# Where the weights begin: a three-pass fp32r loop with its weight tiles moved to multiples of 128 bytes

## The chip, the cores and the metric

One core of one Trainium2 chip runs one program: an attention over 12,480 rows with 32 inducing points, and two multi-layer perceptrons behind it. The metric is the time of one execution on the device, in microseconds (us). The kernel before took 996.77 us as the median of 3 runs (994.26 to 998.2).

An address in this document is the byte at which a tile begins within a partition of SBUF, the on-chip memory. "32 past" means that this address leaves 32 when it is divided by 128.

## The reference, cut to what matters

```python
def _attn_ref(x, inducing):              # x: 1 x 12480 x 128, inducing: 32 x 128
    def mab(q, kv):
        s = scale * (q @ kv.transpose(0, 2, 1))
        a = np.exp(s - s.max(-1, keepdims=True))
        a /= a.sum(-1, keepdims=True) + 1e-09
        return a @ kv
    h = mab(I, x)                        # 32 x 128
    return mab(x, h)                     # 12480 x 128
def _moe_ref(x, w_in, w_out, alpha):     # w_in: 128 x 2048, w_out: 2048 x 128
    h = x @ w_in
    g = np.maximum(h, 0.0) + alpha * np.minimum(h, 0.0)
    return g @ w_out
def _moe2_ref(x, w_in, w_out):
    h = np.maximum(x @ w_in, 0.0)
    return h * h @ w_out
# out = _moe2_ref(_moe_ref(_attn_ref(x, inducing)))
```

## The kernel before, in words

The rows are cut into 30 tiles of 416. A first part (about the first 60 us) loads x, transposes it into `xT`, computes the first attention over all rows and prepares the weights. Then comes the main loop, one step for each pair of a tile of rows and one of the 16 chunks of 128 hidden units, 480 steps, with three layers of it at work on different tiles at the same time.

In each step TensorE runs ten matmuls on 416 moving columns:

- `l1_a` (L570), one matmul: weights `w1s`, moving `a_s`. Its result goes through a Relu on ScalarE (L574) and a split into a high and a low part, `g1h` and `g1l` (L576, VectorE).
- `l1_b` (L580 to L582 in `three`), three matmuls: `wo_hi` with `g1h`, `wo_lo` with `g1h`, `wo_hi` with `g1l`.
- `l2_a` (the same three lines), weights `w2i_hi` and `w2i_lo`, moving `y1h` and `y1l`.
- `l2_b` (the same three lines), weights `w2o_hi` and `w2o_lo`, moving `g2h` and `g2l` (L620 on ScalarE, L622 on GpSimd).

Once for each tile of rows one more matmul follows (L597, weights `v_s`), and once for every four tiles the second attention puts in its scores (L432). All matmuls of the main loop are in fp32r, a form of fp32 that needs one pass; in the first part fp32 is used, in which each matmul that isn't a transpose stands twice in the trace. Each matmul has its own weight load (PEld in the profile): 128 columns of 4 bytes, thus 512 bytes of each partition, and 416 x 4 = 1,664 bytes of each partition move past it. The order on every engine is that in which the code is written (`manual_schedule`); no planner changes it.

Where the tiles lie follows from the order in which the pool `keep` hands them out. `xT` begins 32 past and has 49,920 bytes, which is 390 x 128. So `w1s` behind it begins 32 past, and as each weight tile has 8,192 bytes (64 x 128), `wo_hi`, `wo_lo`, `w2i_hi`, `w2i_lo`, `w2o_hi` and `w2o_lo` all do; a chunk of 128 columns has 512 bytes, so that each single weight load begins 32 past too. In the first part the last four of these places hold `w_in_sb`, `w_out_sb`, `wiT` and `aw`. `v_s` and `hT` behind them are 32 past as well. The moving tiles (`a_s`, `g1h`, `g1l`, `y1h`, `y1l`, `g2h`, `g2l`) have 1,664 bytes each, 13 x 128, and all begin 64 past, as `ident` does.

The names that the prediction speaks of: `keep_tile` (L63), the place of `xT` and `w1s` (L95 to L102), `make_identity` and `same` on GpSimd (L77 to L86), `three` (L579 to L582).

Of the kernel before, what the change touches and what calls it, by code (L numbers as in the profile page):

```python
# [9 lines left out]
F32 = mybir.dt.float32  # L10
# [15 lines left out]
def attention_then_two_mlps(ctx: ExitStack, tc, x, inducing, w_in, w_out, alpha, w2_in, w2_out, out):  # L26
# [3 lines left out]
    nc = tc.nc  # L30
# [3 lines left out]
    P = 128  # L34
# [6 lines left out]
    keep = ctx.enter_context(tc.tile_pool(name="keep", bufs=1))  # L41
# [21 lines left out]
    def keep_tile(name, shape, dt=F32):  # L63
        return keep.tile(shape, dt, name=name, tag=name)

    f32 = lambda ap: ap.bitcast(F32)


    stage1 = ExitStack()
# [27 lines left out]
    def xt_cols(t):  # L97
        return xT[:, t * T : (t + 1) * T]

    w1s = keep_tile("w1s", [P, DFF], F32R)  # L100
    wo_hi = keep_tile("wo_hi", [P, NCH, P], F32R)
    wo_lo = keep_tile("wo_lo", [P, NCH, P], F32R)  # L102
# [2 lines left out]
    w_out_sb = keep.tile([P, NCH, P], F32, name="w_out_sb", tag="w2i_lo")  # L105
    wiT = keep.tile([P, DFF], F32, name="wiT", tag="w2o_hi")
    aw = keep.tile([P, NCH, P], F32, name="aw", tag="w2o_lo")
    al = keep_tile("al", [P, NCH])
    al1 = keep_tile("al1", [P, NCH])
    v_s = keep_tile("v_s", [P, P], F32R)  # L110
# [144 lines left out]
    nm, e, f, s_g, eT, hb = {}, {}, {}, {}, {}, {}  # L255
# [507 lines left out]
```

## Time and profile before

| | |
|---|---|
| median of 3 runs | 996.77 us (994.26 to 998.2) |
| the profiled execution, its own time | 999.72 us |
| its span, first to last instruction | 996.8 us |
| TensorE matmul, busy | 973.7 us (98%) |
| TensorE weight load, busy | 939.9 us (94%) |
| VectorE / ScalarE / GpSimd, busy | 684.8 / 770.4 / 555.3 us |

The span is 2.9 us shorter than the execution's own time, which has a start and an end around it. Busy TensorE doesn't mean that it works at its peak: the record of one matmul lasts some 350 ns while the next begins after some 187 ns, so matmuls overlap in the trace, and how fast TensorE goes is read from the distance between starts.

### The profile page before, as it was taken

Reading aid. Unit: us, or ns where it says so; the run is one execution under the profiler, and the core shown is the slowest. Engines: PE = TensorE matmul, PEld = TensorE weight load, DVE = VectorE, ACT = ScalarE, POOL = GpSimd, SP = SyncE. Lnnn points to the kernel's source line nnn. Section 1 sums busy time; section 2 is a strip of 40 time slices with the busy share of each in tenths; the row PEclk is TensorE's granted clock in tenths of the full one; section 3 lists DMA queues with packets and bytes.
Section 4 is the critical chain, followed back from the end, with each engine's and each line's share of the span. In section 5 each row is a group of like instructions: output and inputs, shape, how many; then the busy total and the mean of one; then the engine's idle time right before and its main releaser. Section 6 shows DMA issues by size and latency. Waiting matters only on the chain.

```text
span 996.8 us, 16261 instructions
## 1 busy us (share of the span) xinstructions
PE 973.7 (98%) x5423; PEld 939.9 (94%) x5423; DVE 684.8 (69%) x1210; ACT 770.4 (77%) x1607; POOL 555.3 (56%) x518
## 2 busy tenths in 40 slices
PE   7879999999999999999999999999999999999998
PEld 5558999999999999999999999999999999999997
DVE  4688776666766667666776667766677666776667
ACT  4569877777887778877787778877787777787776
POOL 1256966555665556655565555655556555565530
PEclk9889999999999999999999999999999999999999
DMA  8715002000020000100001000010000100010001
GB/s 220 200 56 149 1 9 44 10 7 4 10 44 10 10 1 10 44 10 10 3 10 42 10 9 10 10 35 10 9 9 18 27 10 9 10 27 1 10 9 18
DMA packets 66289, 28.42 MB, mean 29 GB/s; under 512 B 54205, under 2 KB 62061, under 8 KB 66205
## 3 DMA queue, kind: packets, MB, share of 16 engines
q1 hardware_dynamic: 66205, 27.39, 12.1%
q8 instruction: 42, 0.69, 0.3%
q14 instruction: 42, 0.34, 0.1%
HBM read 14.80 MB, written 6.39 MB: 21 GB/s over the span
## 4 chain that ended last, share of the span: by engine, by line
PE 91%; DMA 3%; DVE 2%; ACT 2%; issue 1%; POOL 0%; SPq 0%; ACTq 0%; POOLq 0%; DVEq 0%
PE y L582 18%; PE y L581 18%; PE y L580 17%; PE h L582 9%; PE h L581 9%; PE h L580 9%; PE h L570 9%; DMA xg<-in_x_dram 3%; PE ms L432 1%; PE y L597 1%; PE h L236 0%; DMA raw<-in_moe_w_out_dram 0%; ACT g1h L574 0%; DVE mag L175 0%; DVE g1l L576 0%
## 5 line engine op out<-in xcount | busy, mean ns | idle before, releaser
L622 POOL TENSOR_TENSOR g2l<-sq,g2h 128x416 fp32r<-128x416 f32 x456 | 496.2, 1089 | 343.9 <-ACT g2h L620 206.5
L576 DVE SCALAR_TENSOR_TENSOR g1l<-h,g1h 128x416 fp32r<-128x416 f32 x480 | 282.6, 589 | 221.7 <-ACT g1h L574 217.2
L574 ACT ACTIVATE g1h<-h 128x416 fp32r<-128x416 f32 x480 | 248.3, 518 | 132.9 <-PE h L570 129.9
L614 DVE TENSOR_TENSOR sq<-h,r 128x416 f32<-128x416 f32 x480 | 283.6, 591 | 52.2 <-ACT r L612 3.8
L612 ACT ACTIVATE r<-h 128x416 f32<-128x416 f32 x480 | 249.5, 520 | 53.6 <-PE h L582 7.7
L620 ACT CAST g2h<-sq 128x416 fp32r<-128x416 f32 x480 | 255.6, 532 | 2.3 <-DVE sq L614 2.1
L570 PE MATMUL h<-a_s,w1s 128*128 128x416 f32 (+1 forms) x480 | 170.4, 356 | 4.2 <-DVE g1l L576 2.9
L582 PE MATMUL y<-g2l,w2o_hi 128*128 128x416 f32 x480 | 168.7, 351 | 0.3 <-POOL g2l L622 0.3
L582 PE MATMUL y<-g1l,wo_hi 128*128 128x416 f32 x480 | 168.3, 351 | 0.0
L580 PE MATMUL h<-y1h,w2i_hi 128*128 128x416 f32 x480 | 168.1, 350 | 0.2
L582 PE MATMUL h<-y1l,w2i_hi 128*128 128x416 f32 x480 | 167.9, 350 | 0.2 <-DVE y1l L601 0.2
L581 PE MATMUL y<-g1h,wo_lo 128*128 128x416 f32 x480 | 168.0, 350 | 0.0
L581 PE MATMUL h<-y1h,w2i_lo 128*128 128x416 f32 x480 | 168.0, 350 | 0.0
L581 PE MATMUL y<-g2h,w2o_lo 128*128 128x416 f32 x480 | 168.0, 350 | 0.0
L580 PE MATMUL y<-g1h,wo_hi 128*128 128x416 f32 x480 | 167.7, 349 | 0.0
L580 PE MATMUL y<-g2h,w2o_hi 128*128 128x416 f32 x480 | 167.5, 349 | 0.0
L570 PEld LDWEIGHTS h<-a_s,w1s 128*128 128x128 f32 (+1 forms) x480 | 90.5, 189 | 12.0 <-DVE g1l L576 5.7
L580 PEld LDWEIGHTS h<-y1h,w2i_hi 128*128 128x128 f32 x480 | 90.0, 188 | 2.8 <-DVE sq L614 1.4
L580 PEld LDWEIGHTS y<-g1h,wo_hi 128*128 128x128 f32 x480 | 90.3, 188 | 1.0 <-issue 0.5
L582 PEld LDWEIGHTS y<-g2l,w2o_hi 128*128 128x128 f32 x480 | 90.1, 188 | 1.2 <-POOL g2l L622 0.7
L581 PEld LDWEIGHTS y<-g2h,w2o_lo 128*128 128x128 f32 x480 | 90.1, 188 | 0.9 <-POOL w2o_lo L181 0.3
L581 PEld LDWEIGHTS y<-g1h,wo_lo 128*128 128x128 f32 x480 | 90.3, 188 | 0.5
(127 smaller groups left out, 761.4 us busy)
## 6 DMA issues: line engine op xcount, KB each, us to landing
out_dram<-o SPq DMA_DIRECT2D x120, 52.0 KB
xg<-in_x_dram SPq DMA_DIRECT2D x13, 416.0 KB
raw<-in_moe_w_in_dram SPq DMA_DIRECT2D x8, 512.0 KB
raw<-in_moe_w_out_dram SPq DMA_DIRECT2D x8, 512.0 KB
a_s<-a_hi SPq DMA_DIRECT2D x58, 52.0 KB
a_s<-a_lo SPq DMA_DIRECT2D x58, 52.0 KB
xg<-in_x_dram SPq DMA_DIRECT2D x4, 208.0 KB
ind<-in_inducing_dram SPq DMA_DIRECT2D x1, 16.0 KB
```

Of the source, the lines that this page charges most:

```text
L432: nc.tensor.matmul(b[i * M : (i + 1) * M, :w], hT[:, :M], rhs, start=True, stop=True, tile_position=(0, i * M),)
L570: nc.tensor.matmul(b[:, :T], w1s[: a.shape[0], c * P : (c + 1) * P], a, start=True, stop=True)
L574: nc.scalar.activation(hi, b[:, :T], AF.Relu)
L576: nc.vector.scalar_tensor_tensor(lo, b[:, :T], 0.0, f32(hi), op0=ALU.max, op1=ALU.subtract)
L580: nc.tensor.matmul(b, w_hi, hi, start=start, stop=False)
L581: nc.tensor.matmul(b, w_lo, hi, start=False, stop=False)
L582: nc.tensor.matmul(b, w_hi, lo, start=False, stop=stop)
L597: nc.tensor.matmul(b, v_s[: a.shape[0]], a, start=False, stop=True)
L612: nc.scalar.activation(r, b, AF.Relu)
L614: nc.vector.tensor_tensor(sq, b, r, op=ALU.mult)
L620: nc.scalar.copy(hi, sq)
L622: (nc.vector if i >= total - LAG2 else nc.gpsimd).tensor_tensor(lo, sq, f32(hi), op=ALU.subtract)
```

## The change

Two tiles that nothing reads are put into the pool `keep`: one of 96 bytes in each partition between `xT` and `w1s`, and one of 32 bytes behind the last weight tile. The first moves all weight tiles up from 32 past to a multiple of 128. Both together make 128 bytes, so that everything behind them (`al`, `v_s`, `hT`, and all tiles of the other pools, the moving ones among them) is moved by 128 and stays where it was within its 128 bytes: `v_s` and `hT` 32 past, the moving tiles 64 past. Each of the two tiles is cleared once by GpSimd.

```diff
     f32 = lambda ap: ap.bitcast(F32)
+    pads = []
+
+    def pad(n, pool=None):
+
+        name = f"pad{len(pads)}"
+        pads.append((pool or keep).tile([P, n // 4], F32, name=name, tag=name))
+        nc.gpsimd.memset(pads[-1], 0.0)
...
+    pad(96)
     w1s = keep_tile("w1s", [P, DFF], F32R)
     wo_hi = keep_tile("wo_hi", [P, NCH, P], F32R)
     wo_lo = keep_tile("wo_lo", [P, NCH, P], F32R)
...
     aw = keep.tile([P, NCH, P], F32, name="aw", tag="w2o_lo")
+    pad(32)
     al = keep_tile("al", [P, NCH])
```

The order on TensorE, VectorE, ScalarE and SyncE is that of before; nine lines are added ahead of the main loop, so that what stood at L570 stands at L579. On GpSimd two instructions are new. This is GpSimd's queue at the start of the program before (`ident` and `same` are masks for the first part, `w_in_sb` is the first weight that is put together):

```order
6 masks.py:197 MEMSET ident 128x128
7 masks.py:199 ISA
8 masks.py:199 AFFINE_SELECT ident<-ident 128x128
9 L81 MEMSET same 128x128
10 L83 AFFINE_SELECT same<-same 128x128 x7
11 L176 TENSOR_TENSOR w_in_sb<-mag,raw 128x512 x4
```

And this is the same place with the change:

```order
6 masks.py:197 MEMSET ident 128x128
7 masks.py:199 ISA
8 masks.py:199 AFFINE_SELECT ident<-ident 128x128
9 L88 MEMSET same 128x128
10 L90 AFFINE_SELECT same<-same 128x128 x7
11 L73 MEMSET pad_109 128x24
12 L73 MEMSET pad_118 128x8
13 L185 TENSOR_TENSOR w_in_sb<-mag,raw 128x512 x4
```

The two clearings stand behind `same` and ahead of the first weight; nothing else has moved.

## Rows read from the trace of the kernel before

**Rows 1.** The page: busy time of TensorE, its granted clock, the chain that ended last.
```profile
PE 973.7 (98%) x5423; PEld 939.9 (94%) x5423; DVE 684.8 (69%) x1210; ACT 770.4 (77%) x1607; POOL 555.3 (56%) x518
...
PEclk9889999999999999999999999999999999999999
...
PE 91%; DMA 3%; DVE 2%; ACT 2%; issue 1%; POOL 0%; SPq 0%; ACTq 0%; POOLq 0%; DVEq 0%
```

**Rows 2.** Busy time in stretches: us, each engine with its instructions (x), clock, DMA.
```profile
0.00:100.00 100.00, 82.01 (x667) 60.53 (x668) 66.48 (x146) 67.10 (x154) 38.30 (x43) 0.93 0.57 156
...
400.00:500.00 100.00, 100.00 (x537) 98.65 (x536) 67.76 (x116) 78.38 (x162) 57.72 (x54) 1.00 0.09 18
500.00:600.00 100.00, 100.00 (x537) 98.66 (x536) 66.73 (x115) 78.14 (x162) 58.86 (x55) 1.00 0.08 16
```

**Rows 3.** Groups of equal shape: weight loads; busy us, mean ns, idle before.
```profile
L580 PEld LDWEIGHTS y<-g1h,wo_hi 128*128 128x128 f32 x480 | 90.3, 188 | 1.0 <-issue 0.5
L570 PEld LDWEIGHTS h<-a_s,w1s 128*128 128x128 f32 x464 | 87.1, 188 | 5.5 <-DVE sq L614 4.1 <-DVE g1l L576 1.1
L597 PEld LDWEIGHTS y<-a_s,v_s 128*128 128x128 f32 x29 | 5.4, 187 | 0.0
```

**Rows 4.** Timeline of TensorE in the loop: start, length (us), what.
```profile
500.11 0.35 PE L570 MATMUL h<-a_s,w1s 128*128 128x416 f32 x1
500.11 0.19 PEld L580 LDWEIGHTS h<-y1h,w2i_hi 128*128 128x128 f32 x1
500.30 0.35 PE L580 MATMUL h<-y1h,w2i_hi 128*128 128x416 f32 x1
500.30 0.19 PEld L581 LDWEIGHTS h<-y1h,w2i_lo 128*128 128x128 f32 x1
500.48 0.35 PE L581 MATMUL h<-y1h,w2i_lo 128*128 128x416 f32 x1
...
500.50 0.52 ACT L574 ACTIVATE g1h<-h 128x416 fp32r<-128x416 f32 x1 [0.31 <-PE h L570]
...
501.98 0.35 PE L570 MATMUL h<-a_s,w1s 128*128 128x416 f32 x1
```

**Rows 5.** Timeline after a stall, when TensorE had run empty.
```profile
353.50 0.19 PEld L570 LDWEIGHTS h<-a_s,w1s 128*128 128x128 f32 x1 [0.68 <-DVE sq L614]
353.50 0.46 PE L570 MATMUL h<-a_s,w1s 128*128 128x416 f32 x1
353.61 0.19 PEld L580 LDWEIGHTS h<-y1h,w2i_hi 128*128 128x128 f32 x1
353.80 0.35 PE L580 MATMUL h<-y1h,w2i_hi 128*128 128x416 f32 x1
...
354.00 0.52 ACT L574 ACTIVATE g1h<-h 128x416 fp32r<-128x416 f32 x1 [1.35 <-PE h L570]
```

**Rows 6.** Timeline: eight matmuls on 128 columns, each with its load.
```profile
78.97 1.05 PE L545 MATMUL y<-aw,wiT 128*128 128x128 f32 x8
...
78.79 1.04 PEld L545 LDWEIGHTS y<-aw,wiT 128*128 128x128 f32 x8
```

**Rows 7.** Groups in three short stretches: matmuls with no weight load beside them.
```profile
L582 PE MATMUL y<-g1l,wo_hi 128*128 128x416 f32 x1 | 0.4, 352 | 0.0
...
L582 PE MATMUL y<-g2l,w2o_hi 128*128 128x416 f32 x1 | 0.4, 353 | 0.0
...
L582 PE MATMUL y<-g2l,w2o_hi 128*128 128x416 f32 x1 | 0.3, 345 | 0.0
```

**Rows 8.** Groups from 200 to 900 us: matmuls with a weight load beside them.
```profile
L580 PE MATMUL y<-g1h,wo_hi 128*128 128x416 f32 x367 | 127.9, 349 | 0.0
...
L582 PE MATMUL y<-g1l,wo_hi 128*128 128x416 f32 x368 | 128.8, 350 | 0.0
```

**Rows 9.** TensorE at the lower clock: busy time in a stretch, then the timeline.
```profile
66.30:67.30 1.00, 1.00 (x4) 0.97 (x3) 0.93 (x4) 1.00 (x3) 0.00 (x0) 0.50 0.00 0
...
66.64 0.55 PE L580 MATMUL y<-g1h,wo_hi 128*128 128x416 f32 x1
66.98 0.55 PE L581 MATMUL y<-g1h,wo_lo 128*128 128x416 f32 x1
67.33 0.55 PE L582 MATMUL y<-g1l,wo_hi 128*128 128x416 f32 x1
```

**Rows 10.** Start of the program: GpSimd's timeline, and its waits (us, times, longest).
```profile
1.25 0.20 POOL L81 MEMSET same<- 128x128 f32 x1
1.52 2.45 POOL L83 TENSOR_SCALAR_AFFINE_SELECT same<-same 128x128 f32<-128x128 f32 x7
...
POOL w_in_sb L176 <- DVE mag L175: 34.7, 3, 22.7
```

**Rows 11.** The chain that ended last, in order of time: the longest pieces of the start.
```profile
2.44 4.34 DMA xg<-in_x_dram
6.80 13.42 DMA xg<-in_x_dram
...
27.07 9.68 DMA xg<-in_x_dram
```

## The prediction

> **What bounds the kernel now.** I read the page first: TensorE's matmuls are busy for 98% of the span, the clock stands at its higher level (2.4 GHz) from about the fourth of the forty slices on, and 91% of the chain that ended last is TensorE [rows 1]. So what counts is how fast TensorE takes its matmuls, and what sets that pace. The stretches show that it is the same everywhere in the main loop: 537 and 537 matmuls in two stretches of 100 us, with TensorE busy in all of it [rows 2]. The timeline then gives the pace itself: from the matmul of L570 at 500.11 us to that of the next step at 501.98 us there are ten matmuls, thus 187 ns for each [rows 4]. The loop has 480 x 10 + 30 = 4,830 of them, and 4,830 x 187 ns = 903 us of the span of 996.8 us. VectorE, ScalarE and GpSimd have room (684.8, 770.4 and 555.3 us), and TensorE seldom waits for them.
>
> Three things could set the 187 ns: the 416 columns that move past the weights, the weight load, or the two reading from memory at once. The change touches the second and the third, and leaves the first alone. This is where the prediction is decided.
>
> **The weight load.** Its record lasts 188 ns [rows 3], and at first sight that is the whole pace: a load begins with the matmul before it, and the matmul that needs it begins when it ends [rows 4]. But the record is longer than the time that a load holds the next one up. Where matmuls have only 128 columns, eight loads stand within 1.04 us [rows 6]; one after the other they would take 8 x 188 = 1,504 ns. Less the last record's 188 ns, seven distances make 852 ns, 122 ns for each at most. And where TensorE had run empty, its first load begins at 353.50 us and the next one at 353.61 us, and the matmul behind that at 353.80 us: the load was through after 110 ns, and the pace was 190 ns from there on [rows 5]. So in the loop a load has 187 - 110 = 77 ns of slack. If new addresses make it shorter, the slack grows and no matmul starts sooner; if they make it longer by less than 77 ns, no matmul starts later. I put the load at nothing. It shows only where TensorE has run empty. The loads of L570 have 4.1 us of idle time for L614's sake [rows 3], in waits like that of 0.68 us [rows 5], so about six, with one bare load of 110 ns at each; should a start on a 128-byte line save a fifth of it, since 512 bytes from 32 past one touch five such lines and from a multiple only four, that is 22 ns for each, and under half a microsecond in all.
>
> **The two together.** If a load took memory time from the moving columns beside it, a matmul without a load beside it would be shorter. Three such matmuls, behind which TensorE had to wait, last 352, 353 and 345 ns [rows 7]; those of the loop with a load beside them last 349 and 350 ns [rows 8]. The mean of the three is 350. So the load costs the columns nothing that can be seen. The ends of matmuls are modelled in this profile, which weakens this; but they agree with those who wait for them. ScalarE starts on the result of L570 at 500.50 us, 0.04 us after the end in the record (500.11 + 0.35), and in the case of the empty TensorE at 354.00, 0.04 us after 353.50 + 0.46 [rows 4, 5]. Of a matmul without a load no waiting reader is shown, so that the argument is good, not final.
>
> **What stays open.** The 187 ns aren't the bare columns. At the lower clock (0.50, 1.2 GHz) two matmuls take 67.33 - 66.64 = 0.69 us, 345 ns each [rows 9]; half of it is 172.5 ns, and at the higher clock 187 are needed. So 14.5 ns of each matmul belong to something that shows only at the higher clock, when operands have to come twice as fast. 4,830 x 14.5 ns = 70 us hang on it. It can belong to the moving side (1,664 bytes from 64 past one touch 14 lines of 128 bytes where 13 would do, and this stays as it is), to a fixed cost, or to the place of the weights. By rows 7 and 8 it stays when no load is there, which points to the first two.
>
> The Trainium skill (TensorE: Matmul & The Clock Gate, Back-to-back issue gap) gives the distance of matmuls at the higher clock as columns / 2.4 plus 2.5 ns, which it measured on bf16. That would be 175.8 ns for 416 columns, and the trace has 187, so the page and this kernel differ by 11 ns; if the place of the weights were the reason, the time would come to some 943 us. It is a price for the first rival below, which has one of its own from rows.
>
> **The other parts.** Two clearings come into GpSimd's queue, of 24 and of 8 columns. A clearing of 128 columns takes 0.20 us [rows 10], so both together take between nothing and 0.40 us, and I take 0.2. Behind them GpSimd's next work is the first weight, for which it waits up to 22.7 us [rows 10]; that wait hides them. Without this cover they would cost 0.2 us once. TensorE's first transposes need the mask `ident`, which is done ahead of them. Everything behind the weights moves by 128 bytes, the buffers into which x is loaded too; the start of the chain hangs on these loads, with 4.34, 13.42 and 9.68 us in the three longest pieces [rows 11]. They are 27.4 us, and the trace has no load to another place to compare. I bound it by a tenth of them to both sides, an estimate, 2.7 us, and take nothing.
>
> **The sum.** Weight loads 0, moving columns 0, clearings 0, x 0: the span stays 996.8 us, and the execution 999.72 us, of which 2.9 us lie around the span. The profiled execution stands 2.95 us above the median of the runs shown, 996.77 us; no change in the span gives no change in the median, and I forecast 996.8 us.
>
> **The rivals.**
>
> *The weights' place causes the excess, and the change takes it off.* For it: all weights of the loop begin 32 past one, so the trace holds no other case, and the excess shows only at the higher clock, as trouble in feeding would. Even the load of `v_s`, 32 past as well, has a record like the others, 187 ns [rows 3]. Against it: rows 7 and 8. If the whole excess went, 70 us go and 927 us are left. If it goes by lines, four instead of five for each load, a fifth goes, 2.9 ns for each matmul, 14 us: 983 us. I hold the smaller one for likelier, and give this rival 983 us, with 927 us as its far end.
>
> The Trainium skill (SBUF: State Buffer, Specifications) has lines of 16 bytes in the memory. 32 past and 0 past one both begin such a line, and the load covers 32 of them either way; by this page the time stays at 996.8 us. No run here shows lines of any size.
>
> *The two streams meet, and the kernel gets slower.* Weights and moving columns now begin 64 bytes apart within their 128, where they were 32 apart. If the memory serves the two readers from parts that repeat with 64 bytes, both now begin on the same part, and each load holds up the columns that start with it. A fifth of the present excess, 2.9 ns for each matmul, gives 996.8 + 14 = 1,011 us; another whole excess gives 1,067 us. It decides from 1.0 ns for each matmul on (5 us / 4,830). For it speaks nothing in the trace but that the case doesn't occur there; against it that a load beside a matmul leaves it as long as before.
>
> *The move of everything else by 128 bytes decides,* through the loads of x and of `a_s`: up to 2.7 us to either side, 994 to 999.5 us. It would not be told from no change.
>
> **How the numbers follow.** About 0.5%, 5 us, is what a measurement of this kernel can tell from no change. My forecast, no change, has 0.62, the third rival included. The first rival has 0.23, of which I count two thirds to the smaller price. The second has 0.15, two thirds at the smaller price too. So faster 0.23, same 0.62, slower 0.15. The range should hold 8 in 10: it takes the forecast with the bounds of the loads of x, and the smaller price of the first rival with a little room (0.62 + 0.15), and the beginning of the second up to half of its smaller price (about 0.04): 980 to 1,004 us. By itself the forecast has 992 to 1,001 us.
>
> **What would show it.** If I am right, ten matmuls of a step of the changed kernel again take 1.87 us, a stretch of 100 us again holds 537, and a matmul without a load lasts 345 to 353 ns. If the first rival is right, a step takes 1.84 us (a fifth) or as little as 1.73 us, with TensorE at the higher clock and the loads' distance as short as the matmuls'. If the second is right, a step takes 1.90 us or more and the matmuls themselves are longer, with no more waiting than before. If the record of a load got shorter or longer while the distance of matmuls stayed, the slack is shown. What would make me wrong is a pace that moves by more than 1 ns, whatever the load's own record says. A change at the start alone would show in the first 100 us, with the same pace behind it.

## The result: 0.8% slower, and the profile after

The changed kernel takes 1,005.36 us in the median of 7 runs (1,001.8 to 1,008.85); the kernel before, run beside it, 996.77 us (994.26 to 999.56). The ratio is 1.0083, with a 95% interval of 1.0061 to 1.0106. The forecast was no change, 996.8 us with a range of 980 to 1,004: the time lies above the range, and on the side of the second rival.

The page of the profile after, the lines that answer to [rows 1]: TensorE is as busy as before and the clock is the same; the span has grown from 996.8 to 1,001.6 us.

```profile
span 1001.6 us, 16263 instructions
...
PE 980.6 (98%) x5423; PEld 943.6 (94%) x5423; DVE 685.8 (68%) x1210; ACT 771.6 (77%) x1607; POOL 556.4 (56%) x520
...
PEclk9889999999999999999999999999999999999999
```

The stretches of [rows 2] in the kernel after, with the same columns. TensorE is busy in all of each again, at the same clock, but 533 matmuls fit into 100 us instead of 537.

```profile
400.00:500.00 100.00, 100.00 (x533) 98.23 (x532) 67.05 (x114) 77.72 (x161) 57.55 (x54) 1.00 0.08 16
500.00:600.00 100.00, 100.00 (x533) 98.34 (x532) 66.28 (x114) 77.87 (x162) 59.27 (x55) 1.00 0.09 18
```

The groups from 200 to 900 us of the kernel after, which answer to [rows 8]: the records of the matmuls themselves have means of 349 to 357 ns, where it was 349 to 351, and nothing is idle before them. So there is no new wait; the matmuls are slower.

```profile
L589 PE MATMUL y<-g2h,w2o_hi 128*128 128x416 f32 x365 | 130.4, 357 | 0.0
L590 PE MATMUL y<-g2h,w2o_lo 128*128 128x416 f32 x365 | 129.1, 354 | 0.0
L590 PE MATMUL y<-g1h,wo_lo 128*128 128x416 f32 x365 | 128.2, 351 | 0.0
```

The timeline of one step after, as in [rows 4]. The three matmuls from 502.21 on, whose moving tiles lie 192 past a multiple of 256, take 0.56 us together; the three from 502.77 on, with `g2h` and `g2l` in buffers that lie 64 past one, take 0.57 us.

```profile
502.21 0.35 PE L589 MATMUL y<-g1h,wo_hi 128*128 128x416 f32 x1
...
502.40 0.35 PE L590 MATMUL y<-g1h,wo_lo 128*128 128x416 f32 x1
...
502.58 0.35 PE L591 MATMUL y<-g1l,wo_hi 128*128 128x416 f32 x1
...
502.77 0.35 PE L589 MATMUL y<-g2h,w2o_hi 128*128 128x416 f32 x1
...
502.96 0.35 PE L590 MATMUL y<-g2h,w2o_lo 128*128 128x416 f32 x1
...
503.15 0.35 PE L591 MATMUL y<-g2l,w2o_hi 128*128 128x416 f32 x1
...
503.34 0.34 PE L579 MATMUL h<-a_s,w1s 128*128 128x416 f32 x1
```

One step is too coarse for this. The next table takes all fp32r matmuls on 416 columns from 150 to 950 us. It has the distance from each start to the next, in ns, sorted by where the moving tile lies within 256 bytes (1,664 is 6.5 x 256, so neighbouring buffers of a ring alternate between 64 and 192). Distances over 250 ns are left out; they stand just ahead of and behind the second attention's scores (L432, after the change L441), 12 before and 12 after:

```
                                 moving at 64   moving at 192   all
before (weights at 160 of 256)      188.2           187.1       187.7
after  (weights at   0 of 256)      189.6           188.6       189.1
```

That is 1.40 ns more for each matmul, and 4,830 of them make 6.8 us. The interval of the ratio says 6.1 to 10.6 us. The rest of the median's 8.6 us isn't settled; the runs of one kernel spread over 5 to 7 us. The spans of the two traces differ by only 4.8 us because the part up to the loop's 61st step was 1.2 us shorter in the profiled execution after; from there to the last step the loop takes 797.5 us before and 803.4 after, 5.8 us more for 419 of the 480 steps.

Part of the 1.40 ns stands in few matmuls. Of the 2,139 distances at 192 after, 92 are 210 ns long, and no distance before lies between 195 and 280. All 92 begin at a `g2h` with `w2o_hi`, at 192, 87 of them right behind six matmuls in a row whose moving tiles lie at 64. Without them the column at 192 has 187.6 ns and all have 188.6. One of them:

```profile
170.50 0.38 PE L589 MATMUL y<-g2h,w2o_hi 128*128 128x416 f32 x1
...
170.71 0.36 PE L590 MATMUL y<-g2h,w2o_lo 128*128 128x416 f32 x1
...
170.90 0.35 PE L591 MATMUL y<-g2l,w2o_hi 128*128 128x416 f32 x1
```

The record of the first is longer too (0.38 us, where its neighbours have 0.35), and the timeline shows no wait between them. Why these are so long stays open. The two clearings on GpSimd are in the rows, 0.15 us together, and the first weight still waits 21.9 us for VectorE:

```profile
3.94 0.15 POOL L73 MEMSET pad<- 128x24 f32 x2
...
POOL w_in_sb L185 <- DVE mag L184: 29.6, 3, 21.9
```

### The profile page after: what moved, and what is told of

Same layout as the page of the kernel before. It is cut to its first block, busy times and chain, and to the rows that moved or that the text cites. A ratio compares the mean times of both kernels' runs of the same rounds, so it can differ in the third digit from the quotient of the medians.

```text
span 1001.6 us, 16263 instructions
## 1 busy us (share of the span) xinstructions
PE 980.6 (98%) x5423; PEld 943.6 (94%) x5423; DVE 685.8 (68%) x1210; ACT 771.6 (77%) x1607; POOL 556.4 (56%) x520
## 4 chain that ended last, share of the span: by engine, by line
PE 92%; DVE 3%; DMA 2%; ACT 2%; issue 1%; POOL 0%; SPq 0%; POOLq 0%; ACTq 0%; DVEq 0%
PE y L589 18%; PE y L590 17%; PE y L591 17%; PE h L589 9%; PE h L590 9%; PE h L591 9%; PE h L579 9%; DMA xg<-in_x_dram 1%; PE h L245 1%; DVE mag L184 1%; PE y L606 1%; ACT g1h L583 1%; PE ms L441 0%; PE y L316 0%; DVE g1l L585 0%
## 5 line engine op out<-in xcount | busy, mean ns | idle before, releaser
L579 PE MATMUL h<-a_s,w1s 128*128 128x416 f32 (+1 forms) x480 | 170.8, 357 | 4.3 <-DVE g1l L585 2.9
L589 PE MATMUL y<-g2h,w2o_hi 128*128 128x416 f32 x480 | 171.3, 357 | 0.0
L579 PEld LDWEIGHTS h<-a_s,w1s 128*128 128x128 f32 (+1 forms) x480 | 91.5, 191 | 13.4 <-DVE g1l L585 6.5
L591 PEld LDWEIGHTS h<-y1l,w2i_hi 128*128 128x128 f32 x480 | 90.3, 188 | 1.1 <-DVE y1l L610 0.5
L589 PEld LDWEIGHTS y<-g2h,w2o_hi 128*128 128x128 f32 x480 | 90.7, 189 | 0.5
```

The lines of the kernel that those rows point to most:

```text
L579: nc.tensor.matmul(b[:, :T], w1s[: a.shape[0], c * P : (c + 1) * P], a, start=True, stop=True)
L589: nc.tensor.matmul(b, w_hi, hi, start=start, stop=False)
L591: nc.tensor.matmul(b, w_hi, lo, start=False, stop=stop)
```

## The experiments

Below, the distance D of a matmul is the place where its moving tile begins, less the place where the weights begin that are loaded beside it, within 256 bytes. D is in bytes; the time from one start to the next is in ns. The kernel before has 32 and 160 by turns, the change 64 and 192. Each ratio is to the kernel before, run beside it (996.9 us in the first three experiments on the whole kernel, 997.9 in the last three).

**A bare stream of pairs.** Only matmuls, in 64 blocks of 24, one for each place of the weights and of the moving tile:

```python
for a in LETTERS:            # weights wa..wh: 0, 32, ... 224 past a multiple of 256
    for b in LETTERS:        # moving ma..mh: likewise
        for _ in range(REP):
            nc.tensor.matmul(banks[n % 6][:, :T], w[a], m[b], start=True, stop=True)
```

> A bare stream of fp32r matmuls (128x128 weights, 416 moving columns, the shapes of the main loop), 24 for each of 64 pairs of a weight tile and a moving tile: the weights begin 0, 32, ... 224 past a multiple of 256 bytes (wa to wh), the moving tiles likewise (ma to mh). Nothing else of the reference is computed. Theory A (the place of the moving tile relative to the weights within 256 bytes sets what the load costs the matmul beside it): the distance of two matmuls changes along both axes and is the same along each diagonal; by the trace of the changed kernel it is about 190 to 191 ns for wa with mc and 187 for wa with mg, by that of the kernel before 187 for wf with mc and with mg. Theory B (only the place of the weights within a 128-byte line counts): rows differ, columns don't. Theory C (the moving tile alone, 14 lines against 13): columns differ, rows don't, ma and me give some 173 to 176 ns, all others 187. If all 64 lie within 1 ns of 187, the place of operands counts for nothing in a bare stream, and the change in the kernel came from elsewhere.

The timeline of this run merges each block into one row: start, length, what. The length of a block follows D: `wa` with `md` (D = 96) takes 4.79 us, with `mg` (192) 4.65.

```profile
31.18 4.67 PE L39 MATMUL p<-ma,wa 128*128 128x416 f32 x24
35.70 4.65 PE L39 MATMUL p<-mb,wa 128*128 128x416 f32 x24
40.18 4.69 PE L39 MATMUL p<-mc,wa 128*128 128x416 f32 x24
44.71 4.79 PE L39 MATMUL p<-md,wa 128*128 128x416 f32 x24
49.35 4.72 PE L39 MATMUL p<-me,wa 128*128 128x416 f32 x24
53.91 4.65 PE L39 MATMUL p<-mf,wa 128*128 128x416 f32 x24
58.40 4.65 PE L39 MATMUL p<-mg,wa 128*128 128x416 f32 x24
62.89 4.72 PE L39 MATMUL p<-mh,wa 128*128 128x416 f32 x24
...
85.56 4.79 PE L39 MATMUL p<-me,wb 128*128 128x416 f32 x24
...
126.33 4.79 PE L39 MATMUL p<-mf,wc 128*128 128x416 f32 x24
...
176.30 4.65 PE L39 MATMUL p<-ma,we 128*128 128x416 f32 x24
...
212.50 4.79 PE L39 MATMUL p<-ma,wf 128*128 128x416 f32 x24
```

Three of the last four rows have other weights and other moving tiles, with D = 96 in each, and the same 4.79. In 63 of the 64 blocks the value is the same along the diagonal, within 0.4 ns, and different along rows and columns. The exception is `we` with `ma`, the row at 176.30: D = 128, and 186.7 ns where the seven other blocks of its diagonal have 190.2 (`wa` with `me` above, 4.72 us). All 24 of its matmuls are of one kind, 186 to 189 ns apart, where the other seven go through 184, 192, 194 and 190 by turns or nearly so. So one D can have two paces, and no run shows what picks between them. The mean distance of starts by D, without the first two of each block (at 128 without that one block):

```
D      0      32     64     96     128    160    192    224
ns   188.1  186.7  188.7  193.3  190.2  187.0  186.6  189.8
```

Theory A holds but for that block; B and C fall, since both the rows and the columns of the table run through these values. By this table the kernel before stood at 186.7 and 187.0, two of the three best places; the change went to 188.7 and 186.6. The means of these pairs differ by 0.8 ns, where the loop has 1.40; the last experiment comes back to this.

**Everything else moved, the weights not.**

```diff
-    pad(96)
     w1s = keep_tile("w1s", [P, DFF], F32R)
...
-    pad(32)
+    pad(128)
```

> The weights stay at 32 past, as in the kernel before; one tile of 128 bytes behind the last weight tile moves all that comes later up by 128 bytes, as the change does. Theory A: the moving tiles are half at 64 and half at 192 past a multiple of 256 before and after this, so the same pairs occur: no change, 997 us within 3. Theory B: no change, 997 us. The rival that the move of everything else (load buffers, ring of buffers) made the change slower: 1,005 us.

996.85 us, ratio 0.9995 (0.9976 to 1.0013), and 538 matmuls in the stretch. The move of the other tiles makes no difference that these runs can tell; as a cause of the 8.6 us the third rival is out.

```profile
400.00:500.00 100.00, 100.00 (x538) 98.77 (x537) 67.85 (x116) 78.46 (x163) 57.86 (x54) 1.00 0.08 16
```

**The weights at 128 of 256.**

```diff
-    pad(96)
+    pad(224)
```

> As the change, but the first added tile has 224 bytes in place of 96: the weights begin 128 past a multiple of 256, where the change has them at a multiple of 256; the moving tiles lie as before, half at 64 and half at 192. Theory A: the two kinds of moving tile change roles, the sum is that of the change: 1,003 to 1,008 us, and the matmuls whose moving tile is at 192 are now the longer ones (190 to 191 ns). Theory B: 1,005 us as the change, with no change of roles. If only a multiple of 256 were bad: 997 us.

1,006.39 us, ratio 1.0088 (1.0067 to 1.0109). The roles are changed as theory A has it: moving tiles at 192 now have 189.6 ns, a little less than expected, and those at 64 have 188.6. The 92 distances of 210 ns are there again, now at 64, so they go with the places too.

```profile
400.00:500.00 100.00, 100.00 (x533) 98.22 (x532) 67.03 (x115) 77.67 (x162) 57.47 (x53) 1.00 0.08 16
```

**The moving tiles moved, the weights not.**

```diff
-    pad(96)
     w1s = keep_tile("w1s", [P, DFF], F32R)
...
-    pad(32)
+    pad(64)
```

> The weights stay at 32 past; a tile of 64 bytes behind them moves the moving tiles (and all else behind the weights) to multiples of 128. Theory A: pairs that neither kernel had, distances 96 and 224 within 256; the time can go either way, by the probe's value for wf with ma and with me. Theory B: no change, 997 us. Theory C (a moving tile of 13 lines in place of 14): 187 ns become some 173 to 176, and 4,830 matmuls give 930 to 945 us.

1,007.44 us, ratio 1.0113 (1.0088 to 1.0137), 190.2 ns in the mean. Here the weights lie where they lay before, and moving tiles at multiples of 128 make the kernel slower. The probe's values for the two pairs, 193.3 and 189.8 ns, would have given 191.5. The weights' place alone, theory B, is out.

```profile
400.00:500.00 100.00, 100.00 (x531) 97.66 (x530) 66.89 (x114) 77.42 (x160) 56.12 (x53) 1.00 0.09 17
```

**One distance for all.** The moving buffers get 1,792 bytes, 7 x 256, so that all of them lie 64 past a multiple of 256, and only the weights are put elsewhere. In the second run of this kind the tiles have 128 and 128 bytes (D = 32), in the third 64 and 192 (D = 96):

```diff
+TW = 448
-            a_s[t] = att.tile([P, T], F32R, name="a_s", tag="a_s", bufs=5)
+            a_s[t] = att.tile([P, TW], F32R, name="a_s", tag="a_s", bufs=5)[:, :T]
... (g1h, g1l, y1h, y1l, g2h and g2l likewise)
-    pad(96)
+    pad(224)
```

> All buffers of moving tiles are made 1,792 bytes long in place of 1,664, so that all of them lie at 64 past a multiple of 256; the weights are put 128 past one, so that each moving tile begins 192 past the weights. Theory A: every matmul has the shortest distance of the probe, 186.6 ns, where the kernel before has some 187.6 in the mean: 4,830 x 1.0 ns = 5 us less, 992 us. Theory B (weights at a multiple of 128 are bad by themselves): 1,005 us.

994.37 us, ratio 0.9959 (0.9946 to 0.9973); 186.7 ns in the mean, 540 matmuls in the stretch. The weights lie at a multiple of 128 here too, and this kernel is faster than the change and than the kernel before. Neither operand has a good place of its own.

```profile
400.00:500.00 100.00, 100.00 (x540) 99.03 (x539) 67.80 (x116) 78.68 (x163) 57.65 (x53) 1.00 0.09 17
```

> As the run with 192, but the weights lie 32 past a multiple of 256, so that each moving tile begins 32 past the weights. Theory A: 186.7 ns by the probe, 992 to 993 us. Theory B: 997 us, as the kernel before, whose weights are 32 past a multiple of 128 too.

994.36 us, ratio 0.9967 (0.9952 to 0.9982), and 186.7 ns, the same. The gain of these two is 3 to 4 us where 5 were expected.

> As the run with 192, but the weights lie 224 past a multiple of 256, so that each moving tile begins 96 past the weights, the longest distance of the probe, 193.3 ns. Theory A: 4,830 x (193.3 - 187.6) ns = 28 us more than before, 1,024 us. If the probe does not carry over to the loop, as the run with moving tiles at 96 and 224 suggests in part (191.3 ns there): 1,010 to 1,020 us. If only what lies between 32 and 192 counts: no change.

1,022.52 us, ratio 1.0255 (1.0234 to 1.0276); 193.3 ns in the mean, the probe's value to the tenth, and 522 matmuls in the stretch. Expected were 1,024 us.

```profile
400.00:500.00 100.00, 100.00 (x522) 96.04 (x521) 64.06 (x110) 76.03 (x158) 56.00 (x52) 1.00 0.08 16
```

The groups from 200 to 900 us of this run, loads and matmuls: a load's record is still 187 ns long, shorter than the pace, with 2.1 us of idle time in a group of 357; the matmul's record has grown to 354 to 356 ns. So the load is not late; by its record it is done before the next matmul starts. It is the matmul beside it that gets longer.

```profile
L590 PEld LDWEIGHTS h<-y1h,w2i_hi 128*128 128x128 f32 x357 | 66.9, 187 | 2.1
...
L590 PE MATMUL h<-y1h,w2i_hi 128*128 128x416 f32 x357 | 126.5, 354 | 0.0
```

**What the floor of 187 ns is made of.**

```python
for k in "gd":               # mg: D = 192, md: D = 96
    for cols, wide in [(128, 416), (96, 416), (64, 416), (32, 416),
                       (128, 512), (128, 384), (128, 320), (128, 256)]:
        for _ in range(32):
            nc.tensor.matmul(banks[n % 6][:cols, :wide], w[:, :cols], m[k][:, :wide], ...)
```

> A bare stream of fp32r matmuls as in the first probe, weights (wa) at a multiple of 256, moving tile 192 past it (mg, the shortest distance of the first probe, 186.6 ns) or 96 past it (md, the longest, 193.3 ns); 32 matmuls each with 128, 96, 64 and 32 weight columns on 416 moving columns, then with 128 weight columns on 512, 384, 320 and 256 moving columns. Nothing else of the reference is computed. If the load takes memory time from the moving columns (theory A in full), the excess over 416 / 2.4 = 173.3 ns falls with the weight columns: about 13.3, 10, 6.7 and 3.3 ns for mg, and 20, 15, 10 and 5 for md, and it stays 13.3 and 20 for all moving widths. If the floor of 187 ns belongs to the moving side (14 lines for 13), mg keeps 187 ns for all weight columns, and only the 6.7 ns between mg and md shrink.

Mean distance of starts, ns. The last row is the moving columns divided by the higher clock of 2.4 GHz, an estimate of the bare columns: at half that clock 416 columns took 345 ns [rows 9], and 416 / 1.2 is 347.

```
weights x moving   128x416  96x416  64x416  32x416  128x512  128x384  128x320  128x256
D = 192             186.7   188.7   186.7   187.8    233.4    174.7    146.7    117.8
D = 96              193.3   188.2   190.6   188.1    233.3    176.6    146.7    120.1
moving / 2.4        173.3   173.3   173.3   173.3    213.3    160.0    133.3    106.7
```

Theory A "in full" fails: with a quarter of the weight columns the floor stays at 188 ns. What lies above it depends on the load's size, but not in order: at D = 96 it is 193.3, 188.2, 190.6 and 188.1 ns from 128 down to 32 weight columns, and at D = 192 the row even rises to 188.7 with 96. Fewer weight columns take away most of the 6.7 ns between the places, which speaks for the load as its cause; that the two reads hinder each other in the memory is likely by this, and not shown. All runs have the weights in use and the weights being loaded at the same place, so they don't tell these two apart. Why the values between go up and down isn't shown either. Nor is the floor a fixed cost: above the bare columns stand 11 ns at 256 columns, 13 to 15 at 320 to 416, and 20 at 512 (D = 192). Nor does it come from 14 lines in place of 13, since in the first probe all eight moving places reach 186.6 or 186.7 ns with the right weights. What it is stays open.

**Places that alternate.**

```python
for a, pair in [("f", "cg"), ("a", "cg"), ("f", "ae")]:
    for run in (1, 3):
        for i in range(72):
            mm(a, pair[i // run % 2])
```

> A bare stream as in the first probe, but with two moving tiles that alternate, singly or three by three, as the rings of buffers in the loop make them do: for the places of the kernel before (weights 160 past a multiple of 256, moving 64 and 192), of the change (weights 0, moving 64 and 192) and of the run with moving tiles at multiples of 128 (weights 160, moving 0 and 128). Nothing else of the reference is computed. If the loop's distances come from the places and their order alone, the three by three streams show its means, about 187.5, 189.1 and 190.2 ns, where the mean of the two single streams of the first probe is 186.9, 187.7 and 191.5. If they show the latter, what the loop has more or less comes from waits and the other engines.

Mean distance of starts, ns, without the first six matmuls of each block:

```
                        one by one   three by three   the loop
weights 160, moving 64/192   191.7        187.8          187.7   (before)
weights   0, moving 64/192   190.1        188.9          189.1   (the change)
weights 160, moving 0/128    190.0        189.1          190.2   (moving tiles at multiples of 128)
```

In the first two cases a bare stream in threes gives the loop's mean within 0.2 ns, with no other engine at work; in the third the loop has 1.1 ns more. The agreement of the second is in part luck: sorted by place that stream has 190.7 ns at 64 and 187.0 at 192, where the loop has 189.6 and 188.6, and it has none of the 210 ns. The mean of the two single streams (186.9, 187.7, 191.5) doesn't give the loop's: where places change, the distances differ from those of a steady stream. They can lie below it, as in the third case, or above it: one by one, the two places of the kernel before take 191.7 ns, though each by itself has 187.0 or less. So D gives the pace of a loop with one D, and only the direction and some of the size where places are mixed.

## Why the prediction was wrong, point by point

- *What bounds the kernel*: right. The pace of TensorE sets the time, and a pace that moves by 1.40 ns moves the kernel. It is over the 1 ns that the prediction itself named as what would make it wrong.
- *The weight load at nothing, by its slack*: right as far as it went. In the run with D = 96 the loads have idle time between them and the pace is 193 ns.
- *The two together*: this step failed, and with it the term "moving columns 0" of the sum. "So the load costs the columns nothing that can be seen" was read from matmuls at D = 32 and 160, where a steady stream has 186.7 and 187.0 ns against a best of 186.6. There it was nearly true. It was then carried to places that the trace doesn't hold, where the same load beside the same columns costs up to 6.7 ns; in the changed kernel it was 1.40 ns, 6.8 us over the loop. The modelled ends, which the prediction named as its weak point, are not what failed: at D = 96 the records do get longer, 354 to 356 ns. The trace of before even had the sign: tiles at 64 stood at 188.2 ns and tiles at 192 at 187.1, with distances of 191 to 195 in 501 of 2,151 of the former and 133 of 2,066 of the latter, and I took one mean of 187.
- *The second rival* had the right kind of cause, the place of the two streams relative to each other, and the direction; its lower price was 2.9 ns and 14 us against 1.40 ns and 8.6 us measured. That it came out slower was in part luck, since its rule is wrong. By a period of 64 bytes D = 0, 64, 128 and 192 would be alike and slow; the runs show a period of 256, with 192 the fastest of all and 96, which is no multiple of 64, the slowest. That the memory serves the two from common parts is not shown.
- *The first rival*, a fifth saved by lines of 128 bytes: wrong. Weights at multiples of 128 gave 1,005.4, 1,006.4 and 994.4 us, by where the moving tiles lay, and no one of the 64 pairs of places came below 186.6 ns, so the excess over the bare columns did not go.
- *The third rival, the clearings, x*: right as far as it can be told, 0.9995 (0.9976 to 1.0013) for the move alone with one clearing.
- *What stays open*: the 14.5 ns are not the load's, since 32 weight columns leave them, and not the place of the moving tile, since all eight places reach 186.7 ns. That they belong to the moving side otherwise is likely, as they change with its width, and not shown. "This stays as it is" tempted me to treat all of the pace as settled, where a part on top of it wasn't.
- *The chances*: 0.62 for no change rested on one argument, from records of one pair of places.

## What to carry to other kernels

The weights and the moving tile of a matmul have a place relative to each other, and an aligned start of one of them is no merit by itself: the same weights at a multiple of 128 bytes gave 994 or 1,006 us. Look at the distance of starts sorted by the address of the operands before calling a pace a constant, and mind ring buffers whose length isn't a multiple of 256 bytes, since they mix places: two good ones, 187.0 and 186.7 ns by themselves, gave 191.7 by turns. A bare stream over all pairs of places is one short run, and it gave the loop's pace to 0.1 ns in the three kernels with one D; where places were mixed it didn't.

## What the runs showed of the hardware

For fp32r matmuls of 128 weight columns and 416 moving columns at the higher clock, the distance of starts depends on the place of the moving tile relative to the weights loaded beside it, with a period of 256 bytes (places were tried in steps of 32), from 186.6 ns (192) to 193.3 ns (96). One of 64 pairs left this order (D = 128, 186.7 ns where seven others have 190.2). With 512 and 320 moving columns the two places give the same (233.4 and 233.3, 146.7 and 146.7), with 384 and 256 again not (174.7 and 176.6, 117.8 and 120.1), which I had not expected and can't explain.
